# First contraction block of the first projection issued row tile by row tile, with its weights cut and a row load moved ahead

## The chip, the cores and the metric

One core of one Trainium2 chip. The metric is device time in microseconds (us) of one execution. The profile counts from the start of its own span; the measured time is the span plus about 1.7 us (before: span 226.68, time 228.39). Times are compared through ratios: the mean time of one kernel's fast runs over the mean of the other's fast runs of the same rounds, with a 95% interval. So a ratio is not quite the ratio of the medians that stand beside it. Landings of loads and DMA packets are read from the records of the packed trace, since the views print only medians of them.

## The reference

```python
def reference(A_x, A_wqkv, A_wo, B_x, B_w_gate, B_w_up, B_w_down):   # cut
    x = A_x                                   # [1, 2048, 512] bf16
    xn = _layernorm(x, axis=-1)
    s = _A_ref(xn, A_wqkv, A_wo)              # starts with xn @ wqkv, wqkv [512, 1536]
    g = _silu(_B_ref(xn, B_w_gate, B_w_up, B_w_down))
    return x + s * g
```

What matters is the beginning. Rows of x are normalized over 512 columns and then multiplied by `wqkv`. The contraction runs over the 512 columns in four blocks of 128.

## The kernel before

The kernel works in four chunks of 512 rows, each of four row tiles of 128 (`P`). The change concerns only the first 256 columns (`HQ`: tiles 0 and 1) of the projection of chunk 0. Six pairs of PSUM accumulators (`pairs`: two of v, four of q and k) are kept open across the contraction blocks `dk`. In the text w0 to w3 are the 128-row blocks of `wqkv`, and x2 and x3 the loads of row tiles 2 and 3. Those tiles are transposed in between, so that the second half of the chunk can follow at once as `qkv_ps`.

```python
    for t in (0, 1):
        load_x(t)
    for k in range(NC - 1):
        load_wqkv(k)
    for t in (2, 3):
        load_x(t)
    load_wqkv(NC - 1)
    load_x(TPQ, TPQ)
    for i, (lo, hi) in enumerate(((0, DF // 2), (DF // 2, DF))):
        load_w(wg_sb, B_w_gate, lo, hi)
        load_w(wu_sb, B_w_up, lo, hi)
        load_x((2 + i) * TPQ, TPQ)            # two late loads of four tiles each
    # ... cut ...
    warm_up(4, P)
    rest = range(1, NC)
    first_stats(0)
    first_moments(0)
    first_stats(1)
    first_rstd(0)
    first_moments(1)
    normalize(0)
    to_psum(0)                                # four transposes into one PSUM tile
    from_psum(0, [0])
    from_psum(0, rest)
    warm_up(2, P)
    first_rstd(1)
    normalize(1, [0])
    normalize(1, rest)
    to_psum(1, [0])
    from_psum(1, [0], nc.vector.tensor_copy)
    to_psum(1, rest)
    from_psum(1, rest, nc.vector.tensor_copy)
    for t in (2, 3):
        first_stats(t)
        first_moments(t)
    nc.scalar.preload_act_table(AF.Gelu_apprx_tanh)
    for t in (2, 3):
        first_rstd(t)
        normalize(t)
    for dk in range(NC):
        for n, (fo, ps) in enumerate(pairs):
            for i in range(2):
                nc.tensor.matmul(
                    ps[:, i, :],
                    lhsT=wqkv_sb[:, dk, (fo + i) * P : (fo + i + 1) * P],
                    rhs=xnT[0][:, dk, 0:HQ],
                    start=False,
                    stop=(dk == NC - 1 and i == 1),
                )
            if (dk, n) in ((2, 5), (3, 2)):
                transpose(dk, copy=nc.vector.tensor_copy)
```

The softmax here doesn't subtract the row's maximum and nothing guards it: scores larger than these inputs give would overflow.

## Time and profile before

| | before |
|---|---|
| time, 3 runs | 228.5 us median (228.41 to 228.5) |
| span of the profiled execution | 226.68 us (its time 228.39) |
| busy PE | 98% of the span |
| first matmul of contraction blocks 0, 1, 2 | 6.27, 7.58, 8.89 us |
| transposes of tile 2; first `qkv_ps` matmul | 10.20; 11.98 us |
| landings of w0, w1, w2 | 5.51, 6.52, 7.45 us |
| landings of x2, x3 | 7.76, 8.68 us |

The page's busy shares and chain and the pieces of the first microseconds are shown in the prediction. Here is the stretch that decides, from the timeline of PE (start, busy us, engine, line, operation, output and inputs, count, and in brackets the idle time before and what ended it), and one row of the windows (from, to, length, then busy us and count of PE, PEld, DVE, ACT and POOL; granted clock; DMA share; GB/s).

```profile
7.58 0.60 PE L578 MATMUL v_ps<-xnT,wqkv_sb 128*128 128x256 bf16 x4
...
10.20 0.39 PE L224 MATMUL tr<-ident,xn 128*128 128x128 bf16 x4
...
11.98 1.25 PE L266 MATMUL qkv_ps<-xnT,wqkv_sb 128*128 128x256 bf16 x10
```

```profile
6.00:8.00 2.00, 1.90 (x19) 1.72 (x19) 0.62 (x3) 0.07 (x1) 0.00 (x0) 1.00 1.02 363
```

The first line of the timeline is contraction block 1 (its v part), the second is the visit to tile 2. There is no bracket at 10.20: PE did not wait there.

### The profile page before, as it was taken

The numbers are of one execution on the slowest core, as the hardware profiler recorded it, in microseconds if no ns is written. First come the engines' busy times: TensorE is split into PE (matmuls) and PEld (weight loads), VectorE is DVE, ScalarE is ACT, GpSimd is POOL, SyncE is SP. The second block draws the span as 40 slices with busy tenths as digits, with TensorE's granted clock in tenths as the row PEclk, the third lists the DMA queues.
The fourth block names the chain that finished last, engine by engine and source line by source line (L and its number), as shares of the span: only waits on it lengthen the run. The fifth ranks groups of instructions, "written<-read, shape, count | busy, mean of one in ns | idle before, by whom it ended". The sixth has DMA issues, their size and how long they took to land.

```text
span 226.7 us, 3599 instructions
## 1 busy us (share of the span) xinstructions
PE 221.7 (98%) x1324; PEld 107.0 (47%) x1324; DVE 152.4 (67%) x280; ACT 132.1 (58%) x209; POOL 20.1 (9%) x67
## 2 busy tenths in 40 slices
PE   7999999999999999999999999999999999999993
PEld 4885444444444444444444444444444444444453
DVE  4689971999995489969813859925934448971434
ACT  4488679767631767676752466676763356756210
POOL 1026941000030000320000000000000000000000
PEclk9999999999999999999999999999999999999999
DMA  6999399942049921100219931100208940001002
GB/s 192 375 397 382 82 215 166 315 115 94 7 101 198 184 58 25 23 4 0 93 41 212 184 105 29 25 2 0 92 21 163 199 121 0 0 0 33 0 25 69
DMA packets 30130, 24.64 MB, mean 109 GB/s; under 512 B 10784, under 2 KB 29600, under 8 KB 30112
## 3 DMA queue, kind: packets, MB, share of 16 engines
q1 hardware_dynamic: 30112, 24.41, 45.0%
q8 instruction: 10, 0.16, 0.3%
q14 instruction: 8, 0.07, 0.1%
HBM read 18.74 MB, written 4.34 MB: 102 GB/s over the span
## 4 chain that ended last, share of the span: by engine, by line
PE 96%; DVE 1%; DMA 1%; issue 0%; ACT 0%; DVEq 0%
PE y_ps L460 21%; PE g_ps L266 21%; PE u_ps L266 21%; PE qkv_ps L266 16%; PE s_ps L476 6%; PE L_ps L355 3%; PE o_ps L423 3%; PE qk_ps L578 2%; DMA x_sb<-in_A_x_dram 1%; PE v_ps L578 1%; PE tr L224 1%; DVE stats L187 1%; PE den_ps L375 0%; DVE m L484 0%; DVE mv L190 0%
## 5 line engine op out<-in xcount | busy, mean ns | idle before, releaser
L266 PE MATMUL g_ps<-xnT,wg_sb 128*128 128x512 bf16 x224 | 57.5, 379 | 0.0
L266 PE MATMUL u_ps<-xnT,wu_sb 128*128 128x512 bf16 x224 | 57.5, 379 | 0.0
L460 PE MATMUL y_ps<-wd_sb,h 128*128 128x512 bf16 (+1 forms) x238 | 49.9, 367 | 0.0
L450 ACT ACTIVATE u<-u_ps 128x512 bf16<-128x512 f32 x56 | 33.5, 598 | 16.9 <-PE u_ps L266 16.9
L452 DVE TENSOR_TENSOR h<-ge,u 128x512 bf16<-128x512 bf16 x56 | 23.8, 424 | 29.0 <-ACT u L450 27.3
L448 ACT ACTIVATE ge<-g_ps 128x512 bf16<-128x512 f32 x56 | 33.5, 598 | 16.4 <-PE g_ps L266 16.3
L337 DVE TENSOR_TENSOR pk<-q_sb,k_sb 128x1024 bf16<-128x1024 bf16 (+1 forms) x56 | 38.9, 759 | 4.6 <-ACT k_sb L290 4.6
L409 DVE TENSOR_TENSOR pv<-E,v_arr 128x1024 bf16<-128x1024 bf16 (+1 forms) x48 | 39.7, 862 | 0.0
L266 PE MATMUL qkv_ps<-xnT,wqkv_sb 128*128 128x512 bf16 (+1 forms) x192 | 37.0, 352 | 0.0
L460 PEld LDWEIGHTS <-h 128*128 128x128 bf16 x238 | 23.0, 98 | 25.9 <-issue 1.3
L266 PEld LDWEIGHTS <-wu_sb 128*128 128x128 bf16 x224 | 21.9, 98 | 26.4
L266 PEld LDWEIGHTS <-wg_sb 128*128 128x128 bf16 x224 | 21.7, 98 | 26.3 <-issue 0.8
L468 ACT ACTIVATE sl<-y_ps 128x512 bf16<-128x512 f32 (+1 forms) x17 | 9.7, 572 | 32.6 <-PE y_ps L460 32.6
L266 PEld LDWEIGHTS <-wqkv_sb 128*128 128x128 bf16 x192 | 18.8, 98 | 17.6
L484 DVE TENSOR_TENSOR m<-s_ps,sl 128x512 bf16<-128x512 f32 (+1 forms) x17 | 11.1, 655 | 19.1 <-PE s_ps L476 19.1
L435 DVE TENSOR_TENSOR oT<-o_ps,rb 128x1024 bf16<-128x1024 f32 x8 | 9.4, 1219 | 11.7 <-DMA rb<-rs_d 11.7
L476 PE MATMUL s_ps<-wo_sb,oT 128*128 128x512 bf16 (+1 forms) x68 | 14.8, 366 | 0.0
L204 POOL TENSOR_TENSOR rstd<-rstd,mhalf 128x1 f32<-128x1 f32 x12 | 8.0, 670 | 71.1 <-DVE rstd L201 71.1
L290 ACT ACTIVATE vst<-qkv_ps 128x512 bf16<-128x512 f32 x14 | 8.4, 597 | 3.7 <-PE qkv_ps L266 3.7
L290 ACT ACTIVATE k_sb<-qkv_ps 128x512 bf16<-128x512 f32 x14 | 8.4, 602 | 3.2 <-PE qkv_ps L266 3.2
L290 ACT ACTIVATE q_sb<-qkv_ps 128x512 bf16<-128x512 f32 x14 | 8.3, 603 | 3.0 <-PE qkv_ps L266 3.0
L476 PEld LDWEIGHTS <-oT 128*128 128x128 bf16 x68 | 6.6, 98 | 7.2
(58 smaller groups left out, 126.6 us busy)
## 6 DMA issues: line engine op xcount, KB each, us to landing
v_arr<-vT SPq DMA_DIRECT2D x16, 520.0 KB, 8.4
vT<-vst SPq DMA_DIRECT2D x8, 256.0 KB, 2.3
out_dram<-o_t SPq DMA_DIRECT2D x15, 128.0 KB, 2.7
wg_sb<-in_B_w_gate_dram SPq DMA_DIRECT2D x2, 896.0 KB, 10.0
wu_sb<-in_B_w_up_dram SPq DMA_DIRECT2D x2, 896.0 KB, 10.7
wd_sb<-in_B_w_down_dram SPq DMA_DIRECT2D x1, 1792.0 KB, 10.8
wqkv_sb<-in_A_wqkv_dram SPq DMA_DIRECT2D x4, 384.0 KB, 4.6
x_sb<-in_A_x_dram SPq DMA_DIRECT2D x3, 512.0 KB, 10.3
```

What stands on the lines that cost most here:

```text
L266: nc.tensor.matmul(ps, lhsT=w[:, dk, lo : lo + P], rhs=xnT[j][:, dk, i0 : i0 + n], start=(dk == 0), stop=(dk == NC - 1),)
L290: nc.scalar.activation(out=dst, in_=ps, func=AF.Copy)
L337: nc.vector.tensor_tensor(out=st[j]["pk"][w][:, c0 : c0 + n, :], in0=st[j]["q"][:, c0 : c0 + n, :], in1=k_sb[j][:, c0 : c0 + n, off : off ...
L409: nc.vector.tensor_tensor(out=pv[:, d : d + n, :], in0=st[j]["E"][:, wh, :].unsqueeze(1).to_broadcast([P, n, TQ]), in1=st[j]["va"][:, 4 * ...
L435: nc.vector.tensor_tensor(out=oT[:, g : g + 2, :], in0=st[j]["o"][:, g : g + 2, :], in1=st[j]["rb"][:].unsqueeze(1).to_broadcast([P, 2, TQ ...
L448: nc.scalar.activation(out=ge[:], in_=g_ps[:], func=AF.Gelu_apprx_tanh)
L450: nc.scalar.activation(out=u[:], in_=u_ps[:], func=AF.Copy)
L452: nc.vector.tensor_tensor(out=h[:], in0=ge[:], in1=u[:], op=ALU.mult)
L460: nc.tensor.matmul(y[:], lhsT=st[j][fc][:, tt * P : (tt + 1) * P], rhs=wd_sb[:, fc, cols], start=(fc == 0), stop=(fc == NF - 1),)
L468: nc.scalar.activation(out=sl[:], in_=y[:], func=AF.Silu)
L476: nc.tensor.matmul(s[:], lhsT=st[j]["oT"][:, g, tt * P : (tt + 1) * P], rhs=wo_sb[:, g, cols], start=(g == 0), stop=(g == NC - 1),)
L484: nc.vector.tensor_tensor(out=m[:], in0=s[:], in1=sl[:], op=ALU.mult)
```

## The change

The intent: block 0 needs only the first 128 columns of a normalized tile, and half of it needs only tile 0. So block 0 is issued tile by tile as 24 matmuls of 128 columns, while tile 1 is still being prepared. To let PE and the copies overlap, block 0 of both tiles shares one PSUM bank (`tra`) and the rest another (`trb`). The v columns of w0 are read first, alone, so that the first matmuls find their weights. x2 is loaded ahead of w2, so that DVE can take its statistics earlier.

```diff
-    for t in (0, 1):
-        load_x(t)
-    for k in range(NC - 1):
-        load_wqkv(k)
-    for t in (2, 3):
-        load_x(t)
-    load_wqkv(NC - 1)
+    load_x(0)
+    load_x(1)
+    load_wqkv(0, slice(2 * D, 3 * D))
+    load_wqkv(0, slice(0, 2 * D))
+    load_wqkv(1)
+    load_x(2)
+    load_wqkv(2)
+    load_x(3)
+    load_wqkv(3)
 ... cut: to_psum and from_psum take the PSUM tile as an argument ...
+    def block(dk, ns, i0=0, n=HQ):      # the matmuls of pairs ns, n columns from i0
 ... cut ...
+    tra = mm.tile([P, 2, P], BF16, name="tra", tag="mm")
+    trb = mm.tile([P, 2, (NC - 1) * P], BF16, name="trb", tag="mm")
-    normalize(0)
-    to_psum(0)
-    from_psum(0, [0])
-    from_psum(0, rest)
-    warm_up(2, P)
+    normalize(0, one)
+    to_psum(0, one, tra[:, 0])
+    from_psum(0, one, tra[:, 0])
+    normalize(0, rest)
+    to_psum(0, rest, trb[:, 0])
+    from_psum(0, rest, trb[:, 0])
     first_rstd(1)
-    normalize(1, [0])
+    normalize(1, one)
     normalize(1, rest)
-    to_psum(1, [0])
-    from_psum(1, [0], nc.vector.tensor_copy)
-    to_psum(1, rest)
-    from_psum(1, rest, nc.vector.tensor_copy)
+    block(0, range(2), 0, P)
+    to_psum(1, one, tra[:, 1])
+    from_psum(1, one, tra[:, 1], nc.vector.tensor_copy)
+    block(0, range(2, 6), 0, P)
+    to_psum(1, rest, trb[:, 1])
+    from_psum(1, rest, trb[:, 1], nc.vector.tensor_copy)
+    block(0, range(6), P, P)
 ... cut: statistics and normalization of tiles 2 and 3, unchanged ...
-    for dk in range(NC):
 ... cut ...
+    block(1, range(6))
+    block(2, range(6))
+    transpose(2, nc.vector.tensor_copy)
+    block(3, range(3))
+    transpose(3, nc.vector.tensor_copy)
+    block(3, range(3, 6))
```

More of the change, by code (lines that the diff above doesn't have):

```diff
@@ L96, in load_w, with load_wqkv @@
         )
-    def load_wqkv(k):
-        nc.sync.dma_start(out=wqkv_sb[:, k, :], in_=A_wqkv[k * P : (k + 1) * P, :])
-    for t in (0, 1):
-        load_x(t)
-    for k in range(NC - 1):
-        load_wqkv(k)
-    for t in (2, 3):
-        load_x(t)
-    load_wqkv(NC - 1)
+    def load_wqkv(k, cols=slice(0, 3 * D)):
+        nc.sync.dma_start(out=wqkv_sb[:, k, cols], in_=A_wqkv[k * P : (k + 1) * P, cols])
+    load_x(0)
[7 more added lines that the diff above has]
+    load_wqkv(3)
     load_x(TPQ, TPQ)
@@ L216, in normalize, with to_psum, from_psum @@
         )
-    trs = {}
-    def to_psum(t, cs=range(NC)):
-        if 0 in cs:
-            trs[t] = mm.tile([P, NC * P], BF16, name="tr", tag="mm")
-        for c in cs:
+    def to_psum(t, cs, tr):
+        for n, c in enumerate(cs):
             nc.tensor.transpose(
-                trs[t][:, c * P : (c + 1) * P], xns[t][:, c * P : (c + 1) * P], ident[:]
+                tr[:, n * P : (n + 1) * P], xns[t][:, c * P : (c + 1) * P], ident[:]
             )
-    def from_psum(t, cs=range(NC), copy=None):
+    def from_psum(t, cs, tr, copy=None):
         j, i = divmod(t, TPQ)
@@ L231, in from_psum @@
             xnT[j] = xtp.tile([P, NC, TQ], BF16, name="xnT")
-        c = slice(cs[0], cs[-1] + 1)
-        dst = xnT[j][:, c, i * P : (i + 1) * P]
-        src = trs[t][:].rearrange("p (c n) -> p c n", c=NC)[:, c]
+        dst = xnT[j][:, cs[0] : cs[-1] + 1, i * P : (i + 1) * P]
+        src = tr.rearrange("p (c n) -> p c n", c=len(cs))
         if copy is None:
@@ L240, in transpose @@
     def transpose(t, copy=None):
-        to_psum(t)
-        from_psum(t, copy=copy)
+        tr = mm.tile([P, NC * P], BF16, name="tr", tag="mm")
+        to_psum(t, range(NC), tr[:])
+        from_psum(t, range(NC), tr[:], copy)
     def warm_up(n, cols):
@@ L549 @@
     warm_up(4, P)
-    rest = range(1, NC)
+    def block(dk, ns, i0=0, n=HQ):
+        for b in ns:
+            fo, ps = pairs[b]
+            for i in range(2):
+                nc.tensor.matmul(
+                    ps[:, i, i0 : i0 + n],
+                    lhsT=wqkv_sb[:, dk, (fo + i) * P : (fo + i + 1) * P],
+                    rhs=xnT[0][:, dk, i0 : i0 + n],
+                    start=False,
+                    stop=(dk == NC - 1 and i == 1),
+                )
+    one, rest = [0], range(1, NC)
+    tra = mm.tile([P, 2, P], BF16, name="tra", tag="mm")
+    trb = mm.tile([P, 2, (NC - 1) * P], BF16, name="trb", tag="mm")
     first_stats(0)
@@ L574 @@
         normalize(t)
-    for dk in range(NC):
-        for n, (fo, ps) in enumerate(pairs):
-            for i in range(2):
-                nc.tensor.matmul(
-                    ps[:, i, :],
-                    lhsT=wqkv_sb[:, dk, (fo + i) * P : (fo + i + 1) * P],
-                    rhs=xnT[0][:, dk, 0:HQ],
-                    start=False,
-                    stop=(dk == NC - 1 and i == 1),
-                )
-            if (dk, n) in ((2, 5), (3, 2)):
-                transpose(dk, copy=nc.vector.tensor_copy)
+    block(1, range(6))
[4 more added lines that the diff above has]
+    block(3, range(3, 6))
     for fo, ps in pairs:
```

## The prediction

> **What bounds the kernel now.** I read the page first (busy shares, chain that ended last), then the chain for the first 13 us, the waits of PE before and after 6.3 us, the timeline of the same stretch, and the DMA issues with their times to landing.
>
> ```profile
> PE 221.7 (98%) x1324; PEld 107.0 (47%) x1324; DVE 152.4 (67%) x280; ACT 132.1 (58%) x209; POOL 20.1 (9%) x67
> PE 96%; DVE 1%; DMA 1%; issue 0%; ACT 0%; DVEq 0%
> ```
>
> PE is busy 98% of the span, and 96% of the chain lies on it. So the time is PE's own work plus what PE has to wait for at its two ends. From 6.3 us to the end, the waits of PE name one gap only, and it begins before that window; the rest is back to back. The change touches nothing after 12 us. It can therefore only move the moment from which PE is never idle again, and all later work shifts by as much. These are pieces of the chain (start us, us, what):
>
> ```profile
> 4.66 0.30 ACT std L191
> ...
> 4.99 0.17 DVE rstd L196
> ...
> 5.19 0.32 DVE xn L212
> ...
> 5.56 0.24 PE tr L224
> ...
> 5.82 0.23 DVE xnT L238
> ...
> 6.10 0.33 PE tr L224 x3
> 6.43 0.44 PE v_ps L578 x4
> 6.87 0.87 PE qk_ps L578 x8
> ...
> 10.36 0.22 PE tr L224 x4
> ```
>
> The reader is to see that the first useful matmul waits for row tile 1: its normalization, one transpose, the DVE copy of it, and then three more transposes that were held up by that copy. Row tile 0 has been transposed and partly copied long before (its copies by ACT ran from 5.41 to 6.07), and waits for tile 1. This line of the waits is the hold-up:
>
> ```profile
> PE tr L224 <- DVE xnT L238: 0.3, 1, 0.3
> ```
>
> The second place to look at is tile 2, whose transposes PE meets after contraction blocks 0, 1 and 2. DVE's timeline there:
>
> ```profile
> 7.79 0.69 DVE L187 BATCH_NORM_STATS2 stats<-x_sb 128x6 f32<-128x512 bf16 x1 [0.96 <-DMA x_sb<-in_A_x_dram]
> 8.52 0.18 DVE L190 BATCH_NORM_AGGREGATE mv<-stats 128x2 f32<-128x6 f32 x1
> 8.71 0.69 DVE L187 BATCH_NORM_STATS2 stats<-x_sb 128x6 f32<-128x512 bf16 x1
> 9.43 0.18 DVE L190 BATCH_NORM_AGGREGATE mv<-stats 128x2 f32<-128x6 f32 x1
> 9.53 0.13 DVE L196 RECIPROCAL rstd<-std 128x1 f32<-128x1 f32 x1
> 9.70 0.41 DVE L212 TENSOR_SCALAR xn<-x_sb,mv,rstd 128x512 bf16<-128x512 bf16 x1
> ```
>
> Tile 2 is normalized at 10.11, and PE begins its transposes at 10.20, when block 2 has just been issued. PE doesn't wait, but the slack is under 0.1 us. The normalization of tile 2 stands in DVE's order behind the statistics of tile 3, and those began at 8.71. In the DMA issues, the load of tile 3 (x3) was issued at 3.62 and took 5.1 us to land, so it landed at about 8.7: x3's landing released them, not DVE's previous instruction.
>
> **What the Trainium skill says.**
> 1. "PSUM — Partial Sum Buffer", section "PSUM bank collisions raise a hardware error": no two of TensorE, VectorE and ScalarE may touch one bank of the same partitions at once, even at different columns, so accesses are guarded by bank. The trace agrees: the three later transposes of tile 1 started 0.05 us after DVE's copy out of the same bank ended, though they write other columns. The change puts block 0 of both tiles in one bank and blocks 1 to 3 in another, so this wait goes.
> 2. "TensorE: Matmul & The Clock Gate", section "Back-to-back issue gap": N/2.4 + 2.5 ns for an isolated warm matmul (56 ns at 128 columns), but about 81 ns at 128 columns for a sustained stream of weight load and matmul. The trace before shows 55 to 56 ns between starts in a run of four transposes, each with its own weight load (0.22 us for x4 in the chain), and 109 ns at 256 columns. It has no longer run of 128-column pairs on changing weights.
> 3. "DMA: Bandwidth & Descriptors", section "Queues, rings and completion order": each DMA engine consumes its ring in order, and a copy is complete only when its slowest engine is. The trace agrees in kind: w0, w1 and w2 (the 128-row blocks of wqkv) landed at 5.5, 6.5 and 7.5, in the order of issue, about 1 us each.
>
> **The change, part by part.**
>
> *Split of block 0.* Removed: 12 matmuls of 256 columns, 12 x 109 = 1.31 us. Added: 24 of 128 columns, 24 x 55 = 1.32 us, if the pitch of the transposes holds. PE's work is unchanged; two warm-up matmuls (0.11 us, in idle time) go. What counts is the start. Durations are those of the same instructions in the trace: normalization of 128 columns 0.31, transpose 0.22 from start to result and 0.055 to the next, ACT copy of 128 columns 0.28 and of 384 0.49, DVE copies 0.23 and 0.36. Hand-overs: DVE to PE 0.05 to 0.06, PE to ACT or DVE 0.04, ACT to PE taken as 0.05.
> - Tile 0, block 0: normalized 4.54 to 4.85, transposed 4.91 to 5.13, copied 5.17 to 5.45, first v matmul at 5.50. Before, the copy waited for all four transposes (5.41).
> - Four v matmuls: PE free at 5.72. Tile 1's block 0 is normalized by about 5.57 (the reciprocal in front of it slips 0.06 behind the extra normalization instruction), so its transpose goes at 5.72, ends at 5.94, and is copied by 6.20.
> - Eight q and k matmuls of tile 0: 5.78 to 6.22. Three transposes of tile 1: 6.22 to 6.39, the last ending at 6.55, copied by 6.95. ACT's copy out of the same bank is over at about 6.05, in time.
> - Twelve matmuls of tile 1: 6.39 to 7.04. Block 1 then needs the copy of 6.95, which is just hidden, and starts at 7.04. Before it started at 7.58 (v_ps row of the timeline). Gain up to here: 0.54 us.
>
> *v columns of w0 alone.* They must be there at 5.5. Whole w0 landed at 5.5 before; a third of it, first in the ring, should land near 4.5 (estimate: tile 1's rows landed at 3.3, and 0.128 MB at about 300 GB/s plus the slow first packets adds a microsecond). The other two thirds land where w0 did, at 5.5 to 5.7, and are wanted at 5.73. That is tight but should just do. One more issue costs about 0.45 us of the queue's sequencer, which runs well ahead of the transfers. The packet records show 46 ns for 1 KB, 75 for 1.8 KB and 121 for 3 KB; a row in two pieces takes about 46 + 84 = 130 against 121, with 8 rows per engine 0.07 us more for everything behind.
>
> *x2 ahead of block 2.* x2 lands about one w earlier, at 6.8 instead of 7.76. w2 moves from 7.45 to about 7.9 and is wanted at 8.35, so it stays hidden. But x3 still stands behind all of w0, w1, x2 and w2: the same bytes as before.
>
> *Where the 0.54 us goes.* With blocks 1 and 2 unchanged (2 x 1.31), PE asks for tile 2's transposes at 9.66. The normalized rows are ready 1.41 us after the statistics of tile 3 start (8.71 to 10.11), plus 0.08 to PE. If x3 lands again at 8.68 to 8.75, PE gets them at 10.20 to 10.25 and everything won is waited away. Its landing was, however, late for its place: x2 to x3 took 0.92 us for 128 KB, and the packet records show one packet of x3 that took 385 ns (7.83 to 8.22) on the engine that finished last. Without this accident x3 lands near 8.35, tile 2 is ready at 9.77, PE starts on it at about 9.85, and 0.35 us is kept. From there the sequence (half of block 3, tile 3, the rest) is as before. So PE's continuous stretch starts up to 0.54 us earlier, of which I expect about half to reach the end: 0.25 to 0.3 us of 228.5.
>
> **The rivals.**
> 1. *All of it is kept* (x3 lands before 8.15): 228.0. For it: landings have a spread of some 0.4 us per packet accident, and the ring carries small packets at the start now. Against it: x3 has the same bytes in front.
> 2. *The wait moves to tile 2, nothing is kept*: PE idles some 0.5 us before the transposes of tile 2, for x3 by way of DVE; 228.4 to 228.5. For it: DVE's timeline above and the unmoved place of x3. Against it: only the 385 ns packet, which need not recur. I take a mixture of this and 1 as the centre.
> 3. *The 128-column matmuls run at 81 ns.* Then block 0 takes 24 x 26 ns = 0.62 us more, block 1 starts at about 7.66 and nothing is won: 228.5 to 228.6. Against it: 55 ns in the runs of four transposes.
> 4. *The rest of w0 or w1 lands late* (past 5.73 or 7.04): PE waits 0.1 to 0.4 us in block 0 or 1. Since PE would wait for tile 2 anyway, this costs little more; 228.3 to 228.5.
>
> **Range and chances.** The whole prize is 0.54 us, or 0.24% of 228.5, plus perhaps 0.1 us of luck in landings; the worst that these rivals make is about 0.1 us of loss. Runs before lie between 228.41 and 228.5. So 2% (4.6 us) is out of reach either way. Predicted 228.2 us; range 227.8 to 228.55; chances: faster by over 2% 0.003, within 2% 0.994, slower 0.003.
>
> **What would show it right or wrong.** Right: first block-0 matmul at about 5.5, block 1 at about 7.0 instead of 7.58, starts of the 128-column matmuls 55 ns apart, no wait of PE on DVE's copy between the transposes of tile 1, and a new gap of PE before the transposes of tile 2, ended by DVE's normalization, of 0.2 to 0.5 us. Statistics of tile 2 start near 6.8; those of tile 3 at 8.3 to 8.75, at x3's landing. The first qkv_ps matmul moves from 11.98 to about 11.7. Wrong: if that gap is missing, x3 landed early and the time is at 228.0 or below; if block 1 starts at 7.5 or later, the split itself failed (pitch, or the landing of w0); if the first qkv_ps matmul moves but the time doesn't, something later than 12 us bounds the kernel after all.

## The result, and the profile after

| | before | changed |
|---|---|---|
| time, 6 runs each | 228.53 us (228.41 to 228.82) | 228.91 us (228.59 to 229.36) |
| ratio | | 1.0015 [1.0002, 1.0029] |

The changed kernel is slower by some 0.3 us: well inside 2%, but above the predicted range, and on the other side of zero. The profiled execution of the changed kernel happened to be its slowest (229.36), so its profile shows the effects enlarged. A second profile of the same kernel, of an ordinary execution (228.78), comes below as an experiment.

The page's busy shares and chain:

```profile
PE 222.4 (98%) x1334; PEld 107.3 (47%) x1334; DVE 152.4 (67%) x281; ACT 132.3 (58%) x209; POOL 26.1 (11%) x67
PE 94%; DMA 2%; SPq 1%; DVE 1%; issue 0%; DVEq 0%
```

PE is still the bound, but PE's share of the chain fell from 96% to 94%, and DMA's rose from 1% to 2%. Why, the waits of PE say (engine, line, operation, what it waited for; us in total, times, longest):

```profile
PE v_ps L552 <- DMA wqkv_sb<-in_A_wqkv_dram: 0.4, 1, 0.4
PE tr L222 <- DVE xn L214: 0.3, 1, 0.3
```

The old wait on DVE's copy (xnT) is gone. Two others are there instead. The timeline of PE shows where:

```profile
5.73 0.39 PE L552 MATMUL v_ps<-xnT,wqkv_sb 128*128 128x128 bf16 x4
...
7.30 0.60 PE L552 MATMUL v_ps<-xnT,wqkv_sb 128*128 128x256 bf16 x4
...
9.21 0.61 PE L552 MATMUL v_ps<-xnT,wqkv_sb 128*128 128x256 bf16 x4 [0.44 <-DMA wqkv_sb<-in_A_wqkv_dram]
...
11.04 0.40 PE L222 MATMUL tr<-ident,xn 128*128 128x128 bf16 x4 [0.35 <-DVE xn L214]
...
12.83 0.38 PE L264 MATMUL qkv_ps<-xnT,wqkv_sb 128*128 128x256 bf16 x2
```

Block 1 starts 0.28 us earlier than before (7.30 against 7.58). Block 2 then waits for w2, and the transposes of tile 2 wait for tile 2's normalization. The idle times in brackets are short by some 0.15 us, because the ends of matmuls are modelled; from the pitch of the starts the two waits are 9.21 − (7.30 + 1.31) = 0.60 us and 11.04 − (9.21 + 1.31) = 0.52 us. Together, −0.28 + 0.60 + 0.52 = 0.84, and the first `qkv_ps` matmul moved by 12.83 − 11.98 = 0.85 us. The timeline of DVE shows what held tile 2 up:

```profile
7.22 0.69 DVE L189 BATCH_NORM_STATS2 stats<-x_sb 128x6 f32<-128x512 bf16 x1
...
9.58 0.69 DVE L189 BATCH_NORM_STATS2 stats<-x_sb 128x6 f32<-128x512 bf16 x1 [1.44 <-DMA x_sb<-in_A_x_dram]
...
10.57 0.41 DVE L214 TENSOR_SCALAR xn<-x_sb,mv,rstd 128x512 bf16<-128x512 bf16 x1
```

Tile 2 had its statistics by 7.9, early as intended. DVE then stood idle for x3, which landed at 9.55 (8.68 before), and only behind the statistics of tile 3 does it normalize tile 2. The chain (start us, us, what) takes the same way:

```profile
4.09 5.47 DMA x_sb<-in_A_x_dram
...
9.58 0.70 DVE stats L189
...
11.04 0.40 PE tr L222 x4
```

Last, the window of 6 to 8 us (from, to, length, then busy us and count of PE, PEld, DVE, ACT and POOL; granted clock; DMA share; GB/s), to be held against the row shown of before:

```profile
6.00:8.00 2.00, 2.00 (x34) 1.93 (x31) 1.30 (x4) 0.33 (x1) 0.00 (x0) 1.00 1.06 300
```

The DMA engines were as busy as before (share 1.06 against 1.02) but moved 300 GB/s instead of 363. The packet records show slow ones: six packets of weights (3072 bytes) that began between 6.0 and 6.2 us took 0.5 to 1.8 us each, where 121 ns is the usual time. Summed over the packets, 1.69 MB had been started by 8 us, against 1.93 MB before.

From the first `qkv_ps` matmul to the end of the span it is 214.82 us, against 214.70 before. This 0.12 us was not in the prediction.

So there are three things to explain: the late landings, where the split's gain goes, and the 0.12 us at the end.

### The profile page after: what moved, and what is told of

The parts are those of the page before. It is cut to its first block, busy times and chain, and to the rows that moved or that the text cites. A ratio compares the mean times of both kernels' runs of the same rounds, so it can differ in the third digit from the quotient of the medians.

```text
span 227.7 us, 3622 instructions
## 1 busy us (share of the span) xinstructions
PE 222.4 (98%) x1334; PEld 107.3 (47%) x1334; DVE 152.4 (67%) x281; ACT 132.3 (58%) x209; POOL 26.1 (11%) x67
## 4 chain that ended last, share of the span: by engine, by line
PE 94%; DMA 2%; SPq 1%; DVE 1%; issue 0%; DVEq 0%
PE y_ps L458 21%; PE g_ps L264 21%; PE u_ps L264 21%; PE qkv_ps L264 16%; PE s_ps L474 6%; PE L_ps L353 3%; PE o_ps L421 3%; DMA x_sb<-in_A_x_dram 2%; SPq L100 1%; SPq L88 1%; PE tr L222 0%; PE den_ps L373 0%; PE qk_ps L552 0%; DVE stats L189 0%; PE v_ps L552 0%
## 6 DMA issues: line engine op xcount, KB each, us to landing
wg_sb<-in_B_w_gate_dram SPq DMA_DIRECT2D x2, 896.0 KB, 10.1
```

## The experiments

All kernels below compute correct results. "Split" means block 0 tile by tile with the new PSUM tiles. "Old order" is x0 x1 w0 w1 w2 x2 x3 w3. The first four expectations weigh three theories: the new order of loads costs (1); landings are accidents in either order, and the split only takes away the slack that hid them (2); the split or its 128-column matmuls cost PE time (3). Later ones add the "gate theory" (what sets the time is when tile 2 can be transposed) and a theory of the end of the program.

### The change taken apart: split alone, order alone, half of each

`e1_order_undone` is the changed kernel with the load order of before. `e2_order_alone` is the kernel before with the new loads (w0 in two pieces, x2 ahead of w2). `e3_w0_whole` is the changed kernel with w0 in one piece. `e4_x2_back` is the changed kernel with x2 behind w2, w0 still in two pieces.

```diff
 e1_order_undone, against the changed kernel: the nine load lines become
+    for t in (0, 1):
+        load_x(t)
+    for k in range(NC - 1):
+        load_wqkv(k)
+    for t in (2, 3):
+        load_x(t)
+    load_wqkv(NC - 1)
 e2_order_alone, against the kernel before: its seven load lines become the nine of the change, with the new load_wqkv(k, cols)
 e3_w0_whole, against the changed kernel:
-    load_wqkv(0, slice(2 * D, 3 * D))
-    load_wqkv(0, slice(0, 2 * D))
+    load_wqkv(0)
 e4_x2_back, against the changed kernel:
-    load_x(2)
     load_wqkv(2)
+    load_x(2)
     load_x(3)
```

> The changed kernel with the load order of the kernel before (x0 x1 w0 w1 w2 x2 x3 w3, w0 whole); only the tile-by-tile split of block 0 and the two shared PSUM banks are left. Theory 1 (the new load order is what costs: x and w loads by turns make w2 and x3 land late): w2 lands at 7.4 to 7.9 and x3 at 8.3 to 8.8 as in the kernel before, no wait of PE for w2, tile 2's transposes at 10.1 to 10.2; ratio to before 0.998 to 1.000. Theory 2 (landings are accidents of single packets in either order, the split only takes the slack away that hid them): landings scatter as in the changed kernel, ratio 1.000 to 1.002. Theory 3 (the 128-column matmuls or the split cost PE time): ratio about 1.0015 as in the changed kernel with landings as before.

> The kernel before with the new load order alone (w0 in two pieces, x2 ahead of w2). Theory 1: w2 lands after 8.5, x3 after 9.0, PE waits before block 2 or before tile 2's transposes; ratio 1.001 to 1.003. Theory 2: block 2 is asked for at 8.89 here, so a landing of 7.9 plus an accident is mostly hidden; x3 as in before within its scatter; ratio 0.999 to 1.001. Theory 3: ratio 1.000.

> The changed kernel with w0 read whole again (x2 still ahead of w2). If the split of w0 is the part of the order that costs: landings of w2 and x3 go back by 0.5 us or more against the changed kernel's 9.16 and 9.55, ratio 1.000 or less. If x2 between w1 and w2 costs: w2 still after 8.5, ratio as the changed kernel's 1.0015. First v matmul waits for whole w0 and comes at 5.6 to 5.9 in any case.

> The changed kernel with x2 behind w2 again (w0 still in two pieces). If x2 between w1 and w2 costs: w2 lands at 7.5 to 7.9, x3 at 8.4 to 8.8, ratio 0.998 to 1.000. If the split of w0 costs: w2 and x3 stay late, ratio 1.0015.

Measured on one chip, where the kernel before ran 11 times at 228.80 us (228.33 to 228.92):

| kernel | median (low to high), runs | ratio to before |
|---|---|---|
| e1: split, old loads | 228.54 (228.17 to 229.02), 5 | 0.9994 [0.9981, 1.0006] |
| e2: no split, new loads | 228.94 (228.90 to 229.58), 5 | 1.0016 [1.0004, 1.0028] |
| e3: split, x2 ahead, w0 whole | 228.72 (228.08 to 229.44), 6 | 1.0002 [0.9987, 1.0018] |
| e4: split, x2 back, w0 cut | 228.57 (228.23 to 228.88), 5 | 0.9992 [0.9979, 1.0004] |

The split alone is not slower, so theory 3 falls. The new loads alone, on a kernel without the split, cost what the whole change costs (1.0016 beside 1.0015), above what theory 2 expected (0.999 to 1.001). Putting x2 back, with everything else of the change kept, takes the loss away (0.9992; its interval and the changed kernel's share only 1.0002 to 1.0004), and it shows in the landing of w2: 9.16 in the changed kernel, 8.72 in e2, 7.95 in e4, 7.13 in e1. The windows row of 6 to 8 us for e2, then for e4:

```profile
6.00:8.00 2.00, 1.88 (x19) 1.71 (x19) 1.30 (x4) 0.21 (x2) 0.00 (x0) 1.00 0.88 270
```

```profile
6.00:8.00 2.00, 2.00 (x31) 1.91 (x29) 0.58 (x2) 0.06 (x1) 0.00 (x0) 1.00 0.99 367
```

The low DMA rate goes with the new place of x2, with or without the split and with w0 cut or whole: over all 18 profiles the window gives 253 to 334 GB/s in the ten with x2 ahead of w2, and 328 to 386 in the eight with x2 behind it. With w0 whole but x2 ahead (e3, 1.0002) over half of the way from the changed kernel to e1 and e4 is undone by the ratios, and the runs spread from 228.08 to 229.44. The intervals of all these overlap, so that the cut of w0 has a part of its own is not shown; x2's place alone does go with slower loads.

The cut of w0 also bought nothing that the traces show. With w0 whole the first matmul of block 0 came at 5.42, 5.59 and 5.58 (e3, e1 and later k1), with it cut at 5.50 to 5.73 (changed, e4, later f1 and f2). The expectation of e3, 5.6 to 5.9, was wrong here.

But the old order has a gate of its own, which e1's expectation (tile 2's transposes at 10.1 to 10.2) did not foresee. The timeline of DVE in e1, whose profiled execution was its slowest (229.02):

```profile
8.55 0.69 DVE L187 BATCH_NORM_STATS2 stats<-x_sb 128x6 f32<-128x512 bf16 x1 [1.44 <-DMA x_sb<-in_A_x_dram]
...
10.33 0.41 DVE L212 TENSOR_SCALAR xn<-x_sb,mv,rstd 128x512 bf16<-128x512 bf16 x1
```

Here x2 landed last of the needed (8.52), and DVE's two statistics and two aggregations follow it one after the other. PE had block 2 issued at 8.47 + 1.31 = 9.78 and began the transposes at 10.81: a wait of 1.03 us, in which the split's whole gain (block 1 at 7.17) is lost.

e3's profiled execution (228.08) is the prediction come true, in all but the frequency:

```profile
6.99 0.60 PE L551 MATMUL v_ps<-xnT,wqkv_sb 128*128 128x256 bf16 x4
...
9.86 0.40 PE L221 MATMUL tr<-ident,xn 128*128 128x128 bf16 x4
...
11.65 0.82 PE L263 MATMUL qkv_ps<-xnT,wqkv_sb 128*128 128x256 bf16 x6
```

Block 1 at 6.99 (predicted 7.04), w2 at 7.97 (7.9), x3 at 8.37 (8.35), transposes of tile 2 at 9.86 (9.85), `qkv_ps` at 11.65 (11.7). It needed landings in time (some weight packets took 0.5 to 0.8 us here too, without making w2 late) and a clock that opened early (4.06 us, explained below); the other five runs of e3 took 228.60 to 229.44.

### The change again, and tile 2 taken out from behind tile 3

`f1_changed_again` is the changed kernel itself. `f2_tile2_freed` changes only DVE's and ACT's order: tile 2 is normalized before the statistics of tile 3. `f4_split_x23_early` has the split, w0 whole, the order x0 x1 w0 w1 x2 x3 w2 w3, and f2's order on DVE; `f5_nosplit_x23_early` is the same without the split.

```diff
 f2_tile2_freed, against the changed kernel (f4 and f5 have it too):
     for t in (2, 3):
         first_stats(t)
         first_moments(t)
-    nc.scalar.preload_act_table(AF.Gelu_apprx_tanh)
-    for t in (2, 3):
         first_rstd(t)
         normalize(t)
+    nc.scalar.preload_act_table(AF.Gelu_apprx_tanh)
 f4 (split) and f5 (no split), loads (each loop put on one line here):
+    for t in (0, 1): load_x(t)
+    for k in (0, 1): load_wqkv(k)
+    for t in (2, 3): load_x(t)
+    for k in (2, 3): load_wqkv(k)
```

> The changed kernel itself, for a second profile and more times on a chip shared with the next three. The gate theory (what sets the end is when tile 2 can be transposed, that is x3's landing plus 1.53 us; in every profile so far the span is that moment plus 216.49, or 216.61 where w0 was loaded in two pieces): the span is again the start of tile 2's transposes plus 216.61, within 0.03. If the landings of the first trace (w2 9.16, x3 9.55) were typical of this load order they come back within 0.3; if they were an accident, x3 is at 8.6 to 9.2. Ratio 1.000 to 1.002.

> The changed kernel with DVE's order altered alone: tile 2 is normalized before the statistics of tile 3, so its transposes no longer wait for x3. Gate theory: PE goes through tile 2's transposes without waiting for DVE (9.7, or 1.36 us after w2's landing if that is later), and waits for tile 3 instead, whose transposes start at x3's landing plus about 2.0; the first qkv_ps matmul comes at x3 + 2.9 instead of x3 + 3.3, so 0.3 to 0.4 us less than the changed kernel: ratio 0.998 to 1.000. Rival (the load order or the split cost something elsewhere): ratio as the changed kernel's.

> The split of block 0, w0 whole, both x2 and x3 loaded between w1 and w2, and DVE's order as in the run with tile 2 freed. Gate theory: x3 lands at about 7.3 to 7.8, so neither tile 2 nor tile 3 gates; w2 lands at 8.2 to 9.0 and may make PE wait before block 2. First qkv_ps at 11.4 to 12.0, against about 12.3 typical of the kernel before (its timed runs less 1.71 less 214.70); ratio 0.996 to 0.999. Rival that loads by turns always land late: w2 after 9.2, ratio 1.000 or more.

> The same loads and DVE order as the run before in this call, but the kernel before's unsplit block 0. Gate theory: with the gate at tile 2 gone, block 0's start sets the end, so the split is worth its 0.3 to 0.5 us here though it was worth nothing with the gate: this run is slower than the split one by 0.2 to 0.5 us, its first qkv_ps at 11.95 to 12.1; ratio to before 0.997 to 0.9995. If the two are equal within 0.1, something else than the start of block 0 binds.

Measured on one chip; before there 228.61 us (228.35 to 228.91, 11 runs):

| kernel | median (low to high), runs | ratio to before |
|---|---|---|
| f1: changed kernel | 228.66 (228.50 to 229.72), 6 | 1.0014 [0.9995, 1.0032] |
| f2: changed, tile 2 freed | 228.52 (228.45 to 228.89), 5 | 0.9999 [0.9987, 1.0010] |
| f4: split, x2 and x3 early | 228.31 (228.21 to 228.86), 5 | 0.9993 [0.9980, 1.0006] |
| f5: no split, x2 and x3 early | 228.79 (228.58 to 229.15), 5 | 1.0013 [0.9999, 1.0026] |

f1 repeats the ratio, and shows its make-up: four runs at 228.50 to 228.78 and two at 229.55 and 229.72. A tail above 229.1 stood in every kernel with x2 just ahead of w2 and tile 2 behind tile 3 (changed, e2, e3, f1, later g5), and no run of before lies above 228.94. (Two runs of f5, at 229.12 and 229.15, and g4 below pass 229.1 too.) Most of the loss is in this tail: of the twelve runs of the changed kernel (six here, six in the result) four lie above 229.1, at 229.46 in the mean; the other eight have a mean of 228.68, beside 228.62 of before in the same rounds. The dividing line was drawn after the times were seen. In f1's profile, which has no tail, block 1 starts at 7.36, x3 lands at 8.95, and PE waits 0.45 us before tile 2 (10.44 instead of 9.99). Its first `qkv_ps` matmul comes 0.25 us after that of the profile before, but that profile was one of the fastest runs of before; f1's time (228.78) is an ordinary one for before too.

PE in f1, then in f2:

```profile
10.44 0.40 PE L222 MATMUL tr<-ident,xn 128*128 128x128 bf16 x4 [0.29 <-DVE xn L214]
```

```profile
9.98 0.39 PE L222 MATMUL tr<-ident,xn 128*128 128x128 bf16 x4
...
11.42 0.40 PE L222 MATMUL tr<-ident,xn 128*128 128x128 bf16 x4 [0.20 <-DVE xn L214]
```

f2 takes out only the step in which tile 2 stands behind x3. In its profile x3 is as late as 9.46, yet PE is at tile 2 at 9.98 and waits later, at tile 3. From the landing of x3 to the first `qkv_ps` matmul it takes 12.33 − 9.46 = 2.87 us in f2, and 3.28 us in f1 and in the changed kernel. So x3 still holds PE up, by way of tile 3, but 0.41 us less. f2 has no tail, and its mean is 0.35 us below f1's (228.59 against 228.94). The traces show the way from x3 through DVE and tile 2 to PE; that the loss in time goes this way is supported by the means, but not settled, since the intervals of f1 and f2 overlap. f4 against f5: with that gate partly out, the split is worth 228.88 − 228.45 = 0.43 us of the means (the two intervals share 0.9999 to 1.0006). f5's ratio to before missed the expected 0.997 to 0.9995, and f4's just missed 0.996 to 0.999; why f5 came out no faster than before stays open.

### One load more, and six more: the 0.12 us at the end

In the trace, the end of every kernel is a row of six closing waits on SyncE, 0.06 us apart, in fixed order; together they ask for the eight semaphores that the DMAs take in turn. In the kernel before, the last store is on a semaphore of the second wait, and four waits follow after its landing. One DMA more ahead of it moves it to the first, so that five follow. The theory: w0 in two pieces costs 0.12 us at the end, by being one DMA more. `g1_one_more_load` tests this on the kernel before, by cutting its last x load in two; `g3_x23_early_six` cuts the two late x loads into four pieces each, which is six DMAs more and should put the last store at the end of the row. g3 also has f4's load order with the old order of DVE.

```diff
 g1_one_more_load, against the kernel before:
-        load_x((2 + i) * TPQ, TPQ)
+        load_x((2 + i) * TPQ, TPQ - i)
+        if i:
+            load_x(4 * TPQ - 1)
 g3_x23_early_six (also g4, h1, h2, k1, k2):
-        load_x((2 + i) * TPQ, TPQ)
+        for t in range(TPQ):
+            load_x((2 + i) * TPQ + t)
```

> The kernel before with its last x load cut in two (three tiles and one), nothing else: one DMA more in all, long before the end. Theory of the end (the closing waits go through the eight DMA semaphores in a fixed order, and one more DMA moves the last store to the next of them, so one more wait follows its landing): the time from the first qkv_ps matmul to the end of the span is 214.82, as in the runs with w0 in two pieces, and not 214.70 as in the kernel before. Rival (the 0.12 comes from w0's pieces): 214.70.

> The split of block 0, w0 whole, x2 and x3 between w1 and w2, DVE's order as in the changed kernel, and the two last x loads cut into four each: six DMAs more, which puts the last store on the semaphore that is waited for last. Theory of the end: first qkv_ps to the end of the span 214.40 to 214.50. Gate theory: x3 lands at 7.3 to 8.0, tile 2 is normalized by 9.6, so the gate is w2: tile 2's transposes start at w2's landing plus 1.36, or at 9.7 if that is later. Ratio 0.996 to 0.999. Rival: the cut loads add nothing, 214.70, ratio 0.998 to 1.000.

The last wait of SyncE's queue, in before, g1 and g3 in this order:

```profile
SPq L657 <- DMA out_dram<-o_t: 1.1, 1, 1.1
```

```profile
SPq L659 <- DMA out_dram<-o_t: 1.2, 1, 1.2
```

```profile
SPq L668 <- DMA out_dram<-o_t: 0.9, 1, 0.9
```

From the first `qkv_ps` matmul to the end it is 214.70 to 214.72 us in before and in the five others with as many DMAs (e1, e3, f4, f5, g5), 214.81 to 214.83 in the changed kernel, e2, e4, f1, f2 and g1, and 214.47 to 214.49 in all six kernels with six DMAs more, where no wait follows. In the trace of g1 and of those beside it, 0.06 us are the additional wait, and the last store itself counts as landed 0.04 us later (213.68 or 213.69 us after that matmul, against 213.63 to 213.65 in all others), which I can't explain. The sum agrees in all 18 profiles: one DMA more in the program cost 0.11 to 0.13 us, six more saved 0.21 to 0.23.

g1's single time is of unknown state and is not used. Its profile has another use. The timeline of PE:

```profile
5.06 0.63 PE L226 MATMUL tr<-ident,xn 128*128 128x128 bf16 x4
...
8.09 0.38 PE L580 MATMUL v_ps<-xnT,wqkv_sb 128*128 128x256 bf16 x2
```

The same four transposes took 0.40 us in before, and block 1 started there at 7.58. In g1 they are 107 ns apart instead of 55. The trace records when the throttle opened to full clock: at 3.90 us of the span in before, at 6.74 in g1. In the 16 other profiles it lies anywhere from 3.75 to 6.71. Block 1 started at 7.58 to 8.09 without the split and at 6.99 to 7.75 with it (8.42 in one kernel that waits for w1), later with a later opening. With the split the early matmuls pay for it: in g5, whose clock opened at 6.64, nine starts of block 0 stood 106 or 107 ns apart before, and 55 to 57 ns after. So part of the spread of all these kernels is the phase of the clock, and not their own doing.

g3 took 228.64 us (228.07 to 228.81, 5 runs), ratio 0.9992 [0.9979, 1.0004], beside 228.74 of before on that chip (228.35 to 228.90, 11 runs). I had hoped for more; its profile still waits, in block 2, for w2 (9.40).

### Is the slow stretch a change from rows to weights?

The slow packets of the changed kernel come just after the loads switch from x2 to w2. Theory: a switch from rows to weights costs, so one switch alone (all of x first) should be cheap. `g4_x_first_six` tests it; `g5_w0_whole_again` repeats e3 beside it.

```diff
 g4_x_first_six, against the changed kernel (and six DMAs more, as g3): the nine load lines become
+    for t in range(4):
+        load_x(t)
+    for k in range(NC):
+        load_wqkv(k)
 g5_w0_whole_again: e3 again
```

> As the run before in this call, but all four x tiles are loaded first, then w0 to w3: one change from x to w only. If changes from x to w are what slows the loads: 1.9 MB or more moved by 8 us, as in the orders with x2 behind w2. w0 lands at 5.8 to 6.2 and now gates block 0; w1 to w3 follow about 1 us apart; tile 2's transposes start at 10.0 to 10.3 with no wait for DVE. Ratio 0.997 to 0.999; less scatter from run to run than the changed kernel.

> The changed kernel with w0 whole once more, for a second look at x2 ahead of w2 alone. If this place of x2 costs: several of the first w2 packets take over 0.4 us at about 6 us, at most 1.88 MB moved by 8 us, some runs above 229.0; ratio 1.000 to 1.002. If only both parts of the new order together cost: 1.9 MB or more by 8 us, ratio 0.998 to 1.000.

g4 was the slowest of all: 229.21 us (228.58 to 230.80, 6 runs), ratio 1.0030 [1.0006, 1.0054]. With a single switch it has the slowest packets: eight of w1's, begun at 5.4 to 6.1 us, took 1.1 to 1.6 us, and 1.58 MB had been started by 8 us. That one switch is cheap, and that more switches make it worse, is refuted. g5 took 228.82 us (228.20 to 229.36, 6 runs), ratio 1.0004 [0.9987, 1.0022], as e3, again with a tail (229.29 and 229.36).

### Tile 2 freed, in the old load order

`h1_split_best` and `h2_nosplit_best` have the old load order, six DMAs more, and f2's order on DVE, with and without the split. I thought that these would be the best.

```diff
 h1, against the changed kernel: e1's loads, f2's order on DVE, g3's six DMAs
 h2, against the kernel before: f2's order on DVE, g3's six DMAs
```

> The split of block 0 with the load order of the kernel before, tile 2 normalized before the statistics of tile 3, and the two last x loads cut in four (last store on the semaphore waited for last). If the late loads and the end's waits are the whole cause: first qkv_ps to the end 214.47; tile 3's transposes at x3's landing plus 2.0 or at block 1's start plus 3.5, whichever is later; first qkv_ps at 11.5 to 12.2 by the phase of the clock; mean 228.0 to 228.3, ratio to before 0.9975 to 0.999, and 0.2 to 0.5 us less than the unsplit one. If something else of the split costs, the two are equal and the ratio is 0.999 (the end's waits alone).

> The kernel before with tile 2 freed and the two last x loads cut in four, unsplit. First qkv_ps to the end 214.47; block 1 starts at 7.55 to 8.1 by the phase of the clock, tile 2's transposes 2.6 us after it with no wait; first qkv_ps at 12.0 to 12.5; ratio to before 0.998 to 0.9995.

Missed. h1 took 228.94 us (228.58 to 229.02, 5 runs), ratio 1.0007 [0.9995, 1.0020]; h2 228.85 (228.58 to 229.07, 5 runs), ratio 1.0006 [0.9992, 1.0020]; before there 228.63 (228.46 to 228.83, 9 runs). The profiles say why. f2's order makes tile 3 wait for the whole of tile 2 on DVE and ACT, about 1.8 us per tile, so that tile 3 is ready some 3.75 us after x2's landing. With x2 at 8.1 to 8.2 PE meets tile 3's transposes at 11.85 in h1 and at 11.94 in h2: the gate is now at tile 3, both kernels arrive there, and block 1's lead (7.30 against 8.02) is worth 0.09 us. This was not the wanted gain, but it is the plainest picture of a gain waited away.

### The gate moved to where nobody waits

If the split's gain is lost only at the gate, a kernel in which PE reaches tiles 2 and 3 after they are ready must show it. `k1_split_late_tr` has the split, the old load order, the old order on DVE, six DMAs more, and puts the two transposes 6 and 8 matmuls into block 3. `k2_nosplit_late_tr` is the same without the split.

```diff
 k1_split_late_tr (with e1's loads and g3's six DMAs), against the changed kernel:
-    transpose(2, nc.vector.tensor_copy)
     block(3, range(3))
+    transpose(2, nc.vector.tensor_copy)
+    block(3, range(3, 4))
     transpose(3, nc.vector.tensor_copy)
-    block(3, range(3, 6))
+    block(3, range(4, 6))
 k2_nosplit_late_tr (with the six DMAs), against the kernel before:
-            if (dk, n) in ((2, 5), (3, 2)):
-                transpose(dk, copy=nc.vector.tensor_copy)
+            if (dk, n) in ((3, 2), (3, 3)):
+                transpose(n, copy=nc.vector.tensor_copy)
```

> Split of block 0, load order of the kernel before, transposes of tiles 2 and 3 put 6 and 8 matmuls into block 3, the two last x loads cut in four. Gate theory: block 3 starts at block 1's start plus 2.62 or at w3's landing (9.5 to 9.9) plus 0.05; tile 2's transposes 0.66 later, or at x3 + 1.53 or x2 + 2.3 if that is later; first qkv_ps 1.2 after tile 2's transposes when nothing else waits, so at 11.5 to 12.1; to the end 214.47; ratio to before 0.997 to 0.9985, and 0.2 to 0.5 us below the unsplit one of this pair. Rival (the split gives nothing anywhere): equal to the unsplit one.

> The same without the split. Block 1 starts at 7.55 to 8.1 by the phase of the clock, block 3 at 10.2 to 10.7 with no wait for w3, tile 2's transposes 0.66 later without a wait; first qkv_ps at 12.0 to 12.55; to the end 214.47; ratio to before 0.9985 to 0.9995 (the end's 0.24 us, and the gate's waits in runs where x3 is late).

| kernel | median (low to high), runs | ratio to before |
|---|---|---|
| k1 | 228.25 (228.09 to 228.38), 5 | 0.9973 [0.9961, 0.9986] |
| k2 | 228.81 (228.37 to 228.85), 5 | 0.9990 [0.9976, 1.0004] |
| before, same chip | 228.84 (228.61 to 228.94), 9 | |

The timeline of PE, of k1 and then of k2:

```profile
7.15 0.60 PE L551 MATMUL v_ps<-xnT,wqkv_sb 128*128 128x256 bf16 x4
...
10.70 0.40 PE L221 MATMUL tr<-ident,xn 128*128 128x128 bf16 x4
```

```profile
8.01 0.60 PE L579 MATMUL v_ps<-xnT,wqkv_sb 128*128 128x256 bf16 x4
...
11.28 0.39 PE L225 MATMUL tr<-ident,xn 128*128 128x128 bf16 x4
```

Neither line of the transposes has a bracket, and k1's waits of PE name nothing after its warm-up. k1's starts still leave a gap of about 0.27 us before 10.70 (the two matmuls issued at 10.21 take 0.22), so the gate is nearly out, not wholly: x2 landed at 8.41, and 10.70 is the time at which the rule below lets tile 2 through. By the means the split is worth 228.67 − 228.23 = 0.44 us here (an estimate from the spread of the ten runs gives 0.3 us to either side). (The profiles, 12.12 against 12.63 at the first `qkv_ps` matmul, differ by 0.51, but k1's clock opened at 4.61 and k2's at 6.11.) k1 is the only kernel that is clearly faster than before, by 0.6 us of the means, of which 0.23 is the end waits. It beats the changed kernel too.

### The profiles side by side

Microseconds of the span; "blk 1" and "tr 2" are the starts of contraction block 1 and of the transposes of tile 2; "end" is the time from the first `qkv_ps` matmul (not listed) to the end; MB is what DMA packets had started by 8 us.

| kernel | clock opens | blk 1 | w2 | x2 | x3 | tr 2 | end | MB |
|---|---|---|---|---|---|---|---|---|
| before | 3.90 | 7.58 | 7.45 | 7.76 | 8.68 | 10.20 | 214.70 | 1.93 |
| changed | 5.77 | 7.30 | 9.16 | 7.20 | 9.55 | 11.04 | 214.82 | 1.69 |
| f1 (changed) | 5.09 | 7.36 | 8.60 | 7.66 | 8.95 | 10.44 | 214.81 | 1.69 |
| e1 | 4.94 | 7.17 | 7.13 | 8.52 | 8.87 | 10.81 | 214.70 | 1.99 |
| e2 | 3.75 | 7.59 | 8.72 | 6.91 | 9.09 | 10.58 | 214.82 | 1.68 |
| e3 | 4.06 | 6.99 | 7.97 | 6.47 | 8.37 | 9.86 | 214.70 | 1.85 |
| g5 (as e3) | 6.64 | 7.72 | 8.95 | 6.94 | 9.29 | 10.78 | 214.72 | 1.73 |
| e4 | 4.57 | 7.07 | 7.95 | 8.29 | 8.63 | 10.57 | 214.82 | 1.91 |
| f2 | 5.23 | 7.30 | 8.61 | 7.63 | 9.46 | 9.98 | 214.82 | 1.72 |
| k1 | 4.61 | 7.15 | 8.07 | 8.41 | 8.76 | 10.70 | 214.48 | 1.84 |
| k2 | 6.11 | 8.01 | 7.12 | 8.15 | 8.55 | 11.28 | 214.48 | 1.98 |

In the kernels of the old DVE order (all but f2), tr 2 is the latest of three: PE's own arrival (blk 1 + 2.62, if w2 is in time), x3 + 1.49 (changed, f1, e2, e3, g5), and x2 + 2.28 (e1, e4, k1). In k1 PE's own arrival is later by the six matmuls (0.66 us). The before profile is at a meeting of PE (10.20) and x3 (10.17). This is the rule by which a landing becomes time.

## Why the prediction was wrong

**Block 0 tile by tile: right.** First matmul at 5.50 to 5.73 for the predicted 5.50 where w0 is cut (changed, f1, f2, e4). From there to block 1 it took 1.57 us in the changed kernel and in e3, predicted 1.54. In the changed kernel the 24 matmuls of 128 columns start 55 to 57 ns apart, so rival 3 is out. The wait on DVE's copy between the transposes is gone. The v columns of w0 landed at 4.42 (predicted 4.5) and the rest at 5.67 (5.5 to 5.7). The gain of 0.54 us at block 1 was 0.59 between e3 and before at like opening of the clock (4.06, 3.90), 0.61 between the changed kernel and the unsplit f5 (7.30 and 7.91; clock 5.77 and 5.66), but against the profile before only 0.28 and 0.22 in the two profiles of the changed kernel. Their clock opened 1.2 to 1.9 us later than in the profile before, and in f1 block 1 also sat directly behind w1, which landed at 7.31 (6.52 before). That was rival 4, and cost 7.36 − (5.66 + 1.57) = 0.13 us.

**"x3 still stands behind all of w0, w1, x2 and w2: the same bytes as before": this is the step that failed.** The bytes were the same, and from that I took the same landing, 8.68 to 8.75 or, without one slow packet, 8.35, and w2 at about 7.9 "so it stays hidden". In the four profiles with the change's full load order (changed, f1, e2, f2), x3 landed at 9.55, 8.95, 9.09 and 9.46, and w2 at 9.16, 8.60, 8.72 and 8.61. In the eight profiles with x2 behind w2 (before, e1, e4, g1, h1, h2, k1, k2) x3 landed at 8.10 to 8.87. That the load order does it, and not the split, is shown by e2 (order without split, just as slow) and e4 (x2 back, not slow). So tile 2 could be transposed at 11.04 (changed) or 10.44 (f1), not at the 9.85 of my centre. f2 supports, by its mean and by its profile, that the lateness reaches the end through tile 2.

**"Only the 385 ns packet, which need not recur": wrong reading of one sample.** I took a slow packet of x3 as an accident of a landing that would be better without it. (That it sat on the engine that finished last is not shown: the packet records kept here name no engine.) But 8.68 is an ordinary landing, as the 8.10 to 8.87 above show, and the profiled execution before, at 228.39 us, was one of the fast ones: the kernel before ran 57 times from 228.33 to 228.94 us, and only 14 of these were at 228.50 or below, where all three runs that I had lay. My range was built on the fastest quarter, and had next to no room above.

**The wait moves to tile 2 (rival 2): the right mechanism.** It said "PE idles some 0.5 us before the transposes of tile 2", and 0.52 and 0.45 us were found (changed, f1). I set its time at 228.4 to 228.5, because I let the landing of x3 be as before. That a tail of runs would carry most of the loss, no rival had.

**Block 2 waiting for w2: missed.** I dismissed it with w2 at 7.9 against 8.35 wanted. It cost 0.60 us in the profiled (tail) execution, and nothing in f1, where w2 at 8.60 was wanted at 8.67.

**The end of the program: not in the sum at all.** "From there the sequence (half of block 3, tile 3, the rest) is as before" left out 0.12 us for the additional DMA. g1 shows it alone.

**The phase of the clock: not in the sum.** Over the profiles, block 1 starts up to 0.5 us later without the split and up to 0.8 us later with it when the clock opens late, and so this belongs in the range. My sign "if block 1 starts at 7.5 or later, the split itself failed" was wrong for the same reason: with the split it started at 7.55 to 7.75 in g3, g5 and f4, whose clocks opened at 6.29 to 6.71.

The balance, as an estimate from the ratios, each times 228.7 us: the changed kernel is at +0.34 (1.0015), the split alone at −0.14 (e1), the new loads without the split at +0.37 (e2). So the split gave 0.03 to 0.14 us where the gate stands, and the loads took 0.37 to 0.48, of which 0.12 is at the end. The intervals are about 0.3 us to either side, so of the loads' part only the sign and the rough size are known, and of the split's, where the gate stands, not even the sign. In particular e4, which has the additional DMA, came out no slower than e1; only the profiles show that term.

**What stays open** is why weight packets stall under the new order. In the four profiles with the full new order four to eight packets of weights, begun at 5.8 to 6.3 us, took 0.5 to 1.8 us, and the DMA rate was lower. Such packets are not peculiar to the new order: in the profile before, eleven of w0's, begun at 2.9 to 3.8 us just behind x1, took 0.5 to 1.0 us. So g4 refutes that fewer switches from rows to weights help, but not that such a switch has a part. Whether it is a matter of addresses, of banks or of the pace of issue, no run here tells.

## What to carry to other kernels

Here, work brought forward on the busiest engine was worth little until the next thing that it met was also early: find every later gate, and write down for each the landing at which it would hold, before counting the gain. "Same bytes in front" did not give the same landing, so a reordering of loads is tested by itself, without the change that it is to help. Effects of a few tenths of a microsecond need the spread of many runs first: the one profile and the three times that I started from were among the fastest quarter of what the kernel does.

## What the Trainium skill lacked or had wrong

- "TensorE: Matmul & The Clock Gate", section "Back-to-back issue gap": it gives about 81 ns for a sustained stream of weight load and matmul at 128 columns. Here 24 such pairs with changing weights, among four transposes, started 55 to 57 ns apart once the clock was open (changed kernel), which is its figure for an isolated matmul. A longer stream was not tried.
- The same page, section "What's actually happening", calls the clock's activity window free-running, and says that the transition therefore varies by 500 ns to either side (a note there, of 6 to 14 slow matmuls in one kernel, leaves room for more). The spread was larger: full clock opened at 3.75 to 6.74 us of the span over 18 profiles (of 17 kernels), and block 1 started up to 0.5 us later with it in the kernels without the split. What the window is, no run here tells.
- "DMA: Bandwidth & Descriptors", section "Queues, rings and completion order": it says in which order descriptors are consumed, but nothing of how the order of loads changes the rate. Here, with x2 moved ahead of w2 and w0 in two pieces, single packets of 3072 bytes begun at about 6 us took 0.5 to 1.8 us, and 1.68 to 1.72 MB were started by 8 us (four profiles) instead of 1.84 to 2.03 (eight profiles with x2 behind w2).
- No page that I found has the closing waits on DMA completions: six in a fixed order, 0.06 us each, so that the number of DMAs in a program decides how many come after the last store lands (214.47, 214.70 or 214.82 us for the same work).
